# Windowed attention on one core: a chunk's turned probability blocks in one PSUM bank and moved by one copy, global probabilities turned once for two units, one-bank buffers, another order of the steps

## The chip, the cores and the metric

The kernel runs on one core of a Trainium2 chip. The metric is the device time of one execution in microseconds. Three runs of the kernel before took 964.0, 966.15 and 966.29 us; the median is 966.15 us. One further execution, of 966.44 us, was profiled; its span in the trace is 964.6 us, at a mean granted TensorE clock of 0.992.

## The reference

Three stages follow one another: attention with a local window and 32 global rows, a gated net, and a net with a rational function. All in float32.

```python
B, H, Sl, Sg, D, window = 4, 8, 512, 32, 64, 32
def sm(s):
    e = np.exp(s - np.max(s, axis=-1, keepdims=True))
    return e / (np.sum(e, axis=-1, keepdims=True) + 1e-09)
k_all, v_all = np.concatenate([k_g, k_l], 2), np.concatenate([v_g, v_l], 2)
out_g = np.matmul(sm(q_g @ k_all.T / 8), v_all)            # 32 global queries see all 544 keys
s_ll  = np.where(abs(i - j) <= window, q_l @ k_l.T / 8, -1e9)
out_l = np.matmul(sm([q_l @ k_g.T / 8, s_ll]), v_all)      # 512 local queries: 32 global keys and a window
x = [out_g, out_l]                                         # 2304 tokens x 512
x = (sigmoid(x @ w_gate) * (x @ w_val)) @ w_out            # d_ff 1536
h = x @ w_in                                               # d_ff 2048
g = P(h) / (Q(h) + 1e-6)                                   # cubic over 1 + |b0||h| + |b1|h^2
out = g @ w_out
```

## The kernel before, in words

The attention is cut into 16 units: 4 batches by 4 pairs of heads. A unit has 512 local queries in four chunks of 128, and two heads, `j` = 0 and 1. Each chunk and head sees 224 keys: its own 128, the 32 global ones and two neighbour strips of 32, so a unit's scores are eight blocks of 128 x 224. The 32 global queries of two heads in two neighbouring units are taken together, in the even unit: 4 x 32 = 128 rows by 544 keys.

The steps of a unit `u`, with the name of the function and the engine:

- `s_mm` (TensorE, L201): scores of half a unit (two chunks) into a buffer `pss` of two PSUM banks. `s_max` (VectorE, L210): one custom instruction for each chunk and head reads the scores, subtracts the mask, writes them into `p` and gives the row's maximum. `s_exp` (ScalarE, L217): the exponential with its row sum. `s_add` (GpSimd, L222) adds 1e-9 to the sums, `s_rec` (VectorE, L226) inverts them, `s_norm` (GpSimd, L231) multiplies a chunk of `p`.
- `g_mm` (L239), `g_max` (VectorE, L245), `g_neg` (GpSimd, L249), `g_exp`, `g_add`, `g_rec` (L263), `g_norm` (L267): the same for the global queries, into `pgn`, in even units only.
- `t_mm` (TensorE, L270): for each chunk the probabilities are turned (transposed) into a two-bank buffer `pspt`. Bank 0 takes the own keys of both heads and the chunk's global probabilities, 320 columns; bank 1 takes the 96 other keys, on 96 partitions. `t_own` (VectorE, L291) copies bank 0 into `to`, `t_edge` (ScalarE, L297) copies bank 1 into `te`.
- `v_own` (L306), `v_edge` (L314): the products with the values, into `po` (in the trace `pspv`), two banks for a unit, local and global outputs side by side.
- `x_hi` (ScalarE, L331) writes the outputs rounded to float32r as `xh`, `x_lo` (VectorE, L335) what the rounding left as `xl`, `x_g` (VectorE, L345) adds up the global outputs of the four chunks into `xga`; `x_out` (GpSimd) writes those into `xh` and `xl` once a batch is done.

The order in which the program is written is a table, `STEPS`, of rows (place, name, arguments). Step `name` of unit `u` is written at `u + place`, all sorted by this number, so several units are under way at once; each engine runs its instructions in that order and waits on semaphores. I call the stretch from the first score read of one unit to that of the next a frame. Between them stand the steps `w_raw` to `w_lo`, which load and convert four of the net's weight blocks (place + 3.5 times the block's number). `load`, `g_load` and `c_load` issue DMAs on SyncE's queue, in the same order. `KEPT` says how many units of keys, queries and values are held.

All PSUM buffers of the attention are of one kind, `pair`: four of two banks each, used in turn by `pss`, `psgl`, `pspt` and `po`. Two readers of one such buffer on different engines follow each other, and a buffer is written again only when all readers are done.

After the attention come `gated` (its first matmul is L491) and the rational net, in which each weight is applied as a high and a low part in three matmuls (L491 to L493).

Of the kernel before, what the change touches and what calls it, by code (L numbers as in the profile page):

```python
# [36 lines left out]
def tile_of(tok):  # L37
# [9 lines left out]
    (-3.305, 'load', 'k'),  # L47
    (-3.124, 'load', 'q'),
    (-2.697, 'g_load'),
    (-2.554, 'c_load', 'masks'),  # L50
    (-1.417, 's_mm', 0),
    (-1.371, 'w_raw'),
    (-1.261, 's_max', 0, 1),
    (-1.208, 's_max', 0, 0),
    (-1.023, 'c_load', 'ident'),
    (-0.771, 's_mm', 1),
    (-0.720, 's_max', 1, 0),
    (-0.718, 's_exp', 0, 0),
    (-0.696, 's_max', 1, 1),
    (-0.542, 's_exp', 0, 1),  # L60
    (-0.456, 'g_mm'),
    (-0.370, 'g_max'),
    (-0.257, 's_add', 0),
    (-0.195, 's_exp', 1, 1),
    (-0.192, 'g_neg'),
    (-0.153, 'g_exp'),
    (0.054, 's_exp', 1, 0),
    (0.156, 'load', 'v'),
    (0.164, 'g_add'),
    (0.164, 's_rec', 0),  # L70
# [24 lines left out]
    (1.766, 'v_own', 1),
    (1.780, 'v_edge', 1),
    (1.783, 't_own', 3),
    (1.860, 't_edge', 3),
    (1.864, 'v_own', 2),
    (1.873, 'x_hi', 0),  # L100
    (1.991, 'v_edge', 2),
    (2.040, 'w_hi'),
    (2.070, 'v_own', 3),
    (2.085, 'v_edge', 3),
    (2.103, 'x_g'),
    (2.171, 'x_hi', 1),
    (2.202, 'x_lo', 0),
    (2.203, 'x_lo', 1),
    (2.461, 'w_lo'),
    (2.494, 'x_out'),  # L110
# [28 lines left out]
KEPT = dict(k=4, q=3, v=3, w=3)  # L139


def attention(ctx, tc, ident, xh, xl, ins, other={}, others=0):
# [3 lines left out]
    ps = ctx.enter_context(tc.tile_pool(name="ps", bufs=4, space=PSUM))  # L146

    def pair(name):

        return ps.tile([128, 2, 512], F32, tag="ps", name=name)  # L150
# [10 lines left out]
    for i in range(2):  # L161
        nc.gpsimd.memset(pgn[i][:, S + SG :], 0.0)
# [10 lines left out]
    def load(u, names):  # L173

        b, pr = units[u]
        for x in names:
            shape = {"k": [128, NBLK, WIN], "w": [EDGE, NBLK, 128]}.get(x, [128, NBLK, 128])
            t = st[u][f"{x}n"] = two.tile(shape, F32, tag=f"{x}n", name=f"{x}n{u}", bufs=KEPT[x])
            nc.sync.dma_start(t, ins[f"{x}_l"][b, pr])

# [8 lines left out]
    def s_mm(u, half):  # L189
# [5 lines left out]
        s["sm", half] = two.tile([128, 4], F32, tag="sm", name=f"sm{u}_{half}", bufs=4)  # L195
# [24 lines left out]
    def s_add(u, half):  # L220
        r = st[u]["r", half] = two.tile([128, 4], F32, tag="r", name=f"r{u}_{half}", bufs=4)
        nc.gpsimd.tensor_scalar_add(r, st[u]["sm", half], 1e-9)  # L222

    def s_rec(u, half):
        r = st[u]["r", half]
        nc.vector.reciprocal(r, r)  # L226

    def s_norm(u, half, i):
        p = st[u]["p"][:, 2 * half + i]
        r = st[u]["r", half][:, 2 * i : 2 * i + 2].unsqueeze(2).to_broadcast([128, 2, WIN])  # L230
        nc.gpsimd.tensor_tensor(p, p, r, ALU.mult)  # L231
# [10 lines left out]
    def g_max(u):  # L242
        s = st[u]
        s["gmx"] = two.tile([128, 1], F32, tag="gmx", name=f"gmx{u}")
        nc.vector.tensor_reduce(s["gmx"], s["psg"], mybir.AxisListType.X, ALU.max)  # L245

    def g_neg(u):
        t = st[u]["gmx"]
        nc.gpsimd.tensor_scalar_mul(t, t, -0.125)  # L249
# [7 lines left out]
    def g_add(u):  # L257
        r = st[u]["gr"] = two.tile([128, 1], F32, tag="gr", name=f"gr{u}")
        nc.gpsimd.tensor_scalar_add(r, st[u]["gsm"], 1e-9)

    def g_rec(u):
        r = st[u]["gr"]
        nc.vector.reciprocal(r, r)  # L263

    def g_norm(u):
        n = pgn[u // 2 % 2][:, 0 : S + SG]
        nc.gpsimd.tensor_tensor(n, n, st[u]["gr"].to_broadcast([128, S + SG]), ALU.mult)  # L267

    def turn(out, src):
        nc.tensor.matmul(out, src, ident, is_transpose=True, start=True, stop=True, skip_group_check=True)  # L270

    def t_mm(u, c):

        s = st[u]
        s["pt", c] = ps = pair(f"pspt{u}_{c}")
        g = pgn[u // 2 % 2]
        gat = 128 if u % 2 == 0 else 64
        turn(ps[:, 0, gat : gat + 128], g[:, c * 128 : (c + 1) * 128])
        turn(ps[:, 0, 0:128], s["p"][:, c, 0, 0:128])
        turn(ps[:, 0, 192:320], s["p"][:, c, 1, 0:128])  # L280
        at = 128
        if c == 0:
            turn(ps[0:EDGE, 1, gat : gat + 128], g[:, S : S + EDGE])
            at = 192
        turn(ps[0:EDGE, 1, 0:128], s["p"][:, c, 0, 128:WIN])
        turn(ps[0:EDGE, 1, at : at + 128], s["p"][:, c, 1, 128:WIN])

    def t_own(u, c):
        s = st[u]
        s["to", c] = t = two.tile([128, 320], F32, tag="to", name=f"to{u}_{c}", bufs=3)  # L290
        nc.vector.tensor_copy(t, s["pt", c][:, 0, 0:320])  # L291

    def t_edge(u, c):
        s = st[u]
        n = 320 if c == 0 else 256
        s["te", c] = t = two.tile([EDGE, 320], F32, tag="te", name=f"te{u}_{c}", bufs=3)
        nc.scalar.copy(t[:, 0:n], s["pt", c][0:EDGE, 1, 0:n])  # L297

    def v_own(u, c):

        s = st[u]
        if c == 0:
            s["po"] = pair(f"pspv{u}")
        for j in range(2):
            rows, at = slice(64 * j, 64 * j + 64), 192 * (c % 2) + 32 * (1 - j)
            nc.tensor.matmul(s["po"][rows, c // 2, at : at + 160], s["vn"][:, c, rows], s["to", c][:, 160 * j : 160 * j + 160],  # L306
                             start=True, stop=False)

    def v_edge(u, c):
        s = st[u]  # L310
        n = 160 if c == 0 else 128
        for j in range(2):
            rows, at = slice(64 * j, 64 * j + 64), 192 * (c % 2) + (32 * (1 - j) if c == 0 else 32)
            nc.tensor.matmul(s["po"][rows, c // 2, at : at + n], s["wn"][:, c, rows], s["te", c][:, n * j : n * j + n],  # L314
                             start=False, stop=True)

    def x_parts(u, half):

        b, pr = units[u]
        for c in range(2 * half, 2 * half + 2):  # L320
# [5 lines left out]
            src = st[u]["po"][:, half, 0:384].rearrange("p (c t) -> p c t", t=192)[:, c % 2 : c % 2 + n, 32:160]  # L326
# [11 lines left out]
    xga = [one.tile([128, NPAIR, SG], F32, name=f"xga{i}") for i in range(2)]  # L338

    def x_g(u):  # L340
        b, pr = units[u]
        for j in range(2):
# [487 lines left out]
```

## Time and profile before

| | us |
|---|---|
| median of three runs | 966.15 |
| profiled execution | 966.44 |
| its span | 964.6 |
| TensorE busy in the span | 926.8 (96%) |
| VectorE busy | 687.8 (71%) |
| ScalarE busy | 579.7 (60%) |
| GpSimd busy | 506.2 (52%) |

The execution's own time is 1.84 us longer than its span. In rows of the trace PE is TensorE's matmuls, PEld its weight loads, DVE VectorE, ACT ScalarE, POOL GpSimd, SP SyncE. A row of the timeline gives the start, the duration, the engine, the line of the program and the tiles, out<-in, of one or (x4) several instructions in a run; its bracket is the idle time of the engine before it and what ended it. The busy shares are means over stages with different limits, so the stages are looked at one by one below.

### The profile page before, as it was taken

How to read it: one execution, taken by the hardware profiler on the slowest of the kernel's cores; microseconds unless marked ns; L12 is line 12 of the kernel's file. 1: busy time of each engine (PE TensorE's matmuls, PEld its weight loads, DVE VectorE, ACT ScalarE, POOL GpSimd, SP SyncE). 2: the span in 40 equal slices, each digit the busy share in tenths (PEclk: the TensorE clock that was granted, in tenths of full speed). 3: DMA queues.
4: the chain of work that ended last, by engine and by line, in shares of the span. 5: the costliest groups of instructions: out<-in, count | busy, mean ns of one | idle time of the engine just before them, and what ended most of it. 6: DMA issues, size and time to landing. Idle time of an engine off the chain costs nothing.

```text
span 964.6 us, 14517 instructions
## 1 busy us (share of the span) xinstructions
PE 926.8 (96%) x5104; PEld 810.0 (84%) x5104; DVE 687.8 (71%) x1324; ACT 579.7 (60%) x1227; POOL 506.2 (52%) x471
## 2 busy tenths in 40 slices
PE   6888888999999999999999999999999999999996
PEld 4666666898898898898998998898889888988894
DVE  5777763567667676676766238987888789878985
ACT  6777763444444444344444348877778787777773
POOL 4666571354444444444454337544466566655763
PEclk8999999999999999999999999999999999999999
DMA  8455320244344343344443321001300220010111
GB/s 292 137 174 173 102 83 23 87 154 132 131 151 155 120 154 131 122 151 131 131 164 133 119 88 45 1 1 66 109 0 23 71 83 1 28 60 1 66 55 66
DMA packets 51917, 94.42 MB, mean 98 GB/s; under 512 B 4356, under 2 KB 25988, under 8 KB 51844
## 3 DMA queue, kind: packets, MB, share of 16 engines
q1 hardware_dynamic: 51844, 93.49, 29.2%
q8 instruction: 40, 0.66, 0.3%
q14 instruction: 33, 0.27, 0.1%
HBM read 72.24 MB, written 21.23 MB: 97 GB/s over the span
## 4 chain that ended last, share of the span: by engine, by line
PE 83%; DVE 6%; ACT 5%; issue 3%; POOL 2%; DMA 0%; SPq 0%; ACTq 0%; DVEq 0%; POOLq 0%
PE rp L685 6%; PE rp L684 6%; PE rp L683 6%; PE rp L493 6%; PE rp L491 6%; PE rp L492 6%; PE pg L492 5%; PE pg L491 5%; PE pg L493 5%; PE pv L493 5%; PE pv L492 5%; PE pv L491 5%; PE p L536 5%; PE p L535 5%; PE p L534 5%
## 5 line engine op out<-in xcount | busy, mean ns | idle before, releaser
L615 POOL TENSOR_TENSOR v<-v,u 128x384 f32<-128x384 f32 (+1 forms) x80 | 96.5, 1206 | 112.6 <-ACT v L611 112.0
L658 POOL TENSOR_TENSOR rgl<-t,rgh 128x384 fp32r<-128x384 f32 (+1 forms) x80 | 96.3, 1204 | 37.3 <-POOL v L615 30.5
L522 ACT CAST gh<-t 128x384 fp32r<-128x384 f32 (+1 forms) x60 | 33.4, 557 | 124.7 <-DVE t L519 123.0
L519 DVE TENSOR_TENSOR t<-pv,t 128x384 f32<-128x384 f32 (+1 forms) x60 | 36.6, 610 | 78.3 <-PE pv L493 74.4
L623 DVE TENSOR_TENSOR t<-rp,t 128x384 f32<-128x384 f32 (+1 forms) x80 | 48.6, 608 | 54.4 <-ACT t L619 53.6
L608 ACT ACTIVATE u<-rp 128x384 f32<-128x384 f32 (+1 forms) x80 | 42.6, 533 | 65.7 <-PE rp L493 65.6
L644 DVE SCALAR_TENSOR_TENSOR v<-v,u 128x384 f32<-128x384 f32 (+1 forms) x80 | 79.1, 988 | 0.0
L648 DVE SCALAR_TENSOR_TENSOR t<-t,co,v 128x384 f32<-128x384 f32 (+1 forms) x80 | 74.1, 926 | 2.8
L231 POOL TENSOR_TENSOR p<-p,r 128x448 f32<-128x448 f32 x64 | 59.6, 938 | 17.7 <-DVE r L226 15.2
L523 DVE TENSOR_TENSOR gl<-t,gh 128x384 fp32r<-128x384 f32 (+1 forms) x60 | 39.5, 658 | 37.4 <-ACT gh L522 37.4
L217 ACT ACTIVATE p<-p,mx 128x224 f32<-128x224 f32 x128 | 60.7, 479 | 6.1 <-DVE mx L210 6.1
L611 ACT ACTIVATE v<-u,co 128x384 f32<-128x384 f32 (+1 forms) x80 | 60.3, 753 | 2.7
L632 ACT ACTIVATE u<-v,co 128x384 f32<-128x384 f32 (+1 forms) x80 | 52.7, 659 | 9.8 <-POOL v L615 9.7
L546 DVE TENSOR_TENSOR gacc<-p,gacc 128x384 f32<-128x384 f32 (+1 forms) x100 | 54.8, 603 | 4.6 <-PE p L536 4.6
L619 ACT ACTIVATE t<-rp,co 128x384 f32<-128x384 f32 (+1 forms) x80 | 55.9, 698 | 0.0
L640 DVE SCALAR_TENSOR_TENSOR v<-v,u 128x384 f32<-128x384 f32 (+1 forms) x80 | 55.3, 692 | 0.0
L627 DVE SCALAR_TENSOR_TENSOR t<-t,co,rp 128x384 f32<-128x384 f32 (+1 forms) x80 | 52.8, 660 | 0.0
L210 DVE CUSTOM_DVE_ANT_0 p<-pss,masks 128x224 f32<-128x224 f32 x128 | 43.0, 385 | 13.2 <-DMA masks<-in_masks 7.1
L636 ACT ACTIVATE u<-u,co 128x384 f32<-128x384 f32 (+1 forms) x80 | 51.9, 648 | 0.0
L654 ACT CAST rgh<-t 128x384 fp32r<-128x384 f32 (+1 forms) x80 | 43.5, 544 | 5.9 <-DVE t L648 5.9
L201 PE MATMUL pss<-kn,qn 64*128 64x224 f32 x256 | 34.6, 395 | 8.7 <-DMA qn<-in_q_l 6.1
L270 PE MATMUL pspt<-ident,p 128*128 128x128 f32 (+1 forms) x256 | 40.8, 280 | 0.0
(564 smaller groups left out, 3133.7 us busy)
## 6 DMA issues: line engine op xcount, KB each, us to landing
raw2in<-in_w_in SPq DMA_DIRECT2D x16, 512.0 KB, 3.7
raw2out<-in_w_out SPq DMA_DIRECT2D x16, 512.0 KB, 3.4
kn<-in_k_l SPq DMA_DIRECT2D x16, 448.0 KB, 4.9
raw1gate<-in_w_gate SPq DMA_DIRECT2D x12, 512.0 KB, 5.4
raw1val<-in_w_val SPq DMA_DIRECT2D x12, 512.0 KB, 3.7
raw1out<-in_w_out SPq DMA_DIRECT2D x12, 512.0 KB, 3.4
out<-racc SPq DMA_DIRECT2D x17, 256.0 KB, 2.0
qn<-in_q_l SPq DMA_DIRECT2D x16, 256.0 KB, 2.7
```

Source lines behind the costliest of these rows:

```text
L217: nc.scalar.activation(p, p, AF.Exp, bias=s["mx", half][:, n : n + 1], scale=-1.0, accum_out=s["sm", half][:, n : n + 1])
L231: nc.gpsimd.tensor_tensor(p, p, r, ALU.mult)
L491: nc.tensor.matmul(ps, wh[:, w], mh[:, k], start=k == 0, stop=False)
L492: nc.tensor.matmul(ps, wh[:, w], ml[:, k], start=False, stop=False)
L493: nc.tensor.matmul(ps, wl[:, w], mh[:, k], start=False, stop=k == 3)
L611: nc.scalar.activation(new(u, "v"), st[u]["u"], AF.Identity, bias=b0, scale=b1)
L615: nc.gpsimd.tensor_tensor(s["v"], s["v"], s["u"], ALU.mult)
L644: nc.vector.scalar_tensor_tensor(s["v"], s["v"], 2.0, s["u"], ALU.subtract, ALU.mult)
L648: nc.vector.scalar_tensor_tensor(s["t1"], s["t1"], a0, s["v"], ALU.add, ALU.mult)
L658: nc.gpsimd.tensor_tensor(s["gl"], s["t1"], s["gh"].bitcast(F32), ALU.subtract)
L683: nc.tensor.matmul(ps, gh[:, w], wh, start=k == 0, stop=False)
L684: nc.tensor.matmul(ps, gh[:, w], wl, start=False, stop=False)
```

## The change

The turned blocks. `t_mm` makes four turns of 128 columns for a chunk, two of the own keys and two of keys 96 to 223, into one bank of a new kind of buffer, `bank` (four of one bank; `pair` now has two). Its second two thus have 128 rows, of which the first 32 repeat own keys; the value tile `wn` has zeros there, in three static tiles. One copy of 512 columns, `t_out`, moves the bank into `to`, on ScalarE for chunks 1 and 3 and on VectorE for 0 and 2.

The global probabilities are turned once for two units (`g_turn`, five turns into two banks) and copied into `to` by `e_own` (VectorE, two copies of 128 columns a unit) and `e_edge` (ScalarE, one of 64 columns).

The outputs of a unit's halves lie in a bank each; `x_g` is a copy of 32 columns for each half, and the two halves are added on GpSimd in `x_out`. The small operations `s_add`, `g_neg` and `g_add` go from GpSimd to VectorE, ahead of the reciprocals and behind the global maximum. All places in `STEPS` are new, the loads' among them.

```diff
-    (-3.305, 'load', 'k'),
-    (-2.554, 'c_load', 'masks'),
+    (-3.328, 'c_load', 'masks'),
+    (-2.228, 'load', 'k'),
...
-    ps = ctx.enter_context(tc.tile_pool(name="ps", bufs=4, space=PSUM))
+    ps = ctx.enter_context(tc.tile_pool(name="ps", bufs=2, space=PSUM))
+    def bank(name):
+        return ps.tile([128, 512], F32, tag="bank", name=name, bufs=4)
+    wn = [one.tile([128, NBLK, 128], F32, name=f"wn{i}") for i in range(3)]
+    for t in wn:
+        nc.gpsimd.memset(t[0 : 128 - EDGE], 0.0)
...
-    def s_add(u, half):
-        r = st[u]["r", half] = two.tile([128, 4], F32, tag="r", name=f"r{u}_{half}", bufs=4)
-        nc.gpsimd.tensor_scalar_add(r, st[u]["sm", half], 1e-9)
     def s_rec(u, half):
-        r = st[u]["r", half]
+        r = st[u]["sm", half]
+        nc.vector.tensor_scalar_add(r, r, 1e-9)
         nc.vector.reciprocal(r, r)
...
+        nc.vector.tensor_scalar_mul(t, t, -0.125)
-    def g_neg(u):
-        t = st[u]["gmx"]
-        nc.gpsimd.tensor_scalar_mul(t, t, -0.125)
...
     def g_rec(u):
-        r = st[u]["gr"]
+        r = st[u]["gsm"]
+        nc.vector.tensor_scalar_add(r, r, 1e-9)
         nc.vector.reciprocal(r, r)
...
+    def g_turn(u):
+        g = pgn[u // 2 % 2]
+        st[u]["go"], st[u]["ge"] = bank(f"psgo{u}"), bank(f"psge{u}")
+        for c in range(NBLK):
+            nc.tensor.transpose(st[u]["go"][:, c * 128 : (c + 1) * 128], g[:, c * 128 : (c + 1) * 128], ident)
+        nc.tensor.transpose(st[u]["ge"][:, 0:128], g[:, S - 128 + EDGE : S + EDGE], ident)
+    def e_own(u):
+        src = st[u - u % 2]["go"].rearrange("p (c h g) -> p c h g", c=NBLK, h=4)[:, :, 2 * (u % 2) : 2 * (u % 2) + 2]
+        for i in range(2):
+            nc.vector.tensor_copy(turned(u)[:, i::2, 0:2, 128 * (1 - i) : 128 * (1 - i) + SG], src[:, i::2])
+    def e_edge(u):
+        at = 64 * (u % 2)
+        src = st[u - u % 2]["ge"][:, at : at + 64].rearrange("p (h g) -> p h g", h=2)
+        nc.scalar.copy(turned(u)[:, 0, 2:4, 128:160], src)
     def t_mm(u, c):
-        s["pt", c] = ps = pair(f"pspt{u}_{c}")
...
+        s["pt", c] = ps = bank(f"pspt{u}_{c}")
+        for j in range(2):
+            nc.tensor.transpose(ps[:, 128 * j : 128 * j + 128], s["p"][:, c, j, 0:128], ident)
+        for j in range(2):
+            nc.tensor.transpose(ps[:, 256 + 128 * j : 384 + 128 * j], s["p"][:, c, j, EDGE:WIN], ident)
-    def t_own(u, c):
-        nc.vector.tensor_copy(t, s["pt", c][:, 0, 0:320])
-    def t_edge(u, c):
-        nc.scalar.copy(t[:, 0:n], s["pt", c][0:EDGE, 1, 0:n])
+    def t_out(u, c):
+        at = SG * (c % 2)
+        src = st[u]["pt", c].rearrange("p (n k) -> p n k", n=4)
+        (nc.scalar.copy if c in T_ACT else nc.vector.tensor_copy)(turned(u)[:, c, :, at : at + 128], src)
     def v_own(u, c):
-        if c == 0:
-            s["po"] = pair(f"pspv{u}")
+        if c % 2 == 0:
+            s["po", c // 2] = bank(f"pspv{u}_{c // 2}")
...
-    def x_g(u):
-            nc.vector.tensor_reduce(xga[b % 2][rows, pr], src, mybir.AxisListType.XY, ALU.add)
+    def x_g(u, half):
+        nc.vector.tensor_copy(xga[b % 2][:, pr, half], st[u]["po", half][:, 128:160])
     def x_out(u):
+            nc.gpsimd.tensor_tensor(g[:, :, 0], g[:, :, 0], g[:, :, 1], ALU.add)
```

The first place is VectorE between the score reads of unit 4 (`pss4`) and of unit 5 (`pss5`); the number behind `to`, `pspt`, `pspv`, `mx`, `r`, `sm` and `p` is the unit, `gmx4` belongs to the global queries of units 4 and 5. Before:

```order
L210 ISA p4_431,mx4_1_503<-pss4_1_502,masks_89 128x224
L210 ISA mx4_1_503 128x1
L291 COPY to2_2_538<-pspt2_2_524 128x320
L245 TENSOR_REDUCE gmx4_564<-psgl4_546 128x1
L226 RECIPROCAL r3_1_531<-r3_1_531 128x4
L210 ISA p5_551,mx5_0_553<-pss5_0_552,masks_89 128x224
```

and now:

```order
L248 TENSOR_REDUCE gmx4_515<-psgl4_502 128x1
L249 TENSOR_SCALAR gmx4_515<-gmx4_515 128x1
L282 COPY to3_522<-psgo2_391 128x2x2x32 x2
L228 TENSOR_SCALAR sm3_1_362<-sm3_1_362 128x4
L229 RECIPROCAL sm3_1_362<-sm3_1_362 128x4
L340 TENSOR_TENSOR xl0_72<-pspv2_0_510,xh0_67 128x256
L347 COPY xga0_102<-pspv2_0_510 128x32
L228 TENSOR_SCALAR sm4_0_441<-sm4_0_441 128x4
L229 RECIPROCAL sm4_0_441<-sm4_0_441 128x4
L259 TENSOR_SCALAR gsm4_539<-gsm4_539 128x1
```

The copies of the turned blocks no longer stand here one by one between the reads; all small operations of a unit stand together, ahead of the next unit's reads.

The second place is TensorE from the value products of unit 2 on. Before:

```order
L306 MATMUL pspv2_561<-to2_3_583,vn2_370 64x160 x2
L314 MATMUL pspv2_561<-te2_3_592,wn2_416 64x128 x2
L270 MATMUL pspt3_0_613<-ident_66,pgn1_91 128x128
L270 MATMUL pspt3_0_613<-ident_66,p3_304 128x128 x2
L270 MATMUL pspt3_0_613<-ident_66,pgn1_91 96x128
L270 MATMUL pspt3_0_613<-ident_66,p3_304 96x128 x2
L270 MATMUL pspt3_1_628<-ident_66,pgn1_91 128x128
L270 MATMUL pspt3_1_628<-ident_66,p3_304 128x128 x2
L270 MATMUL pspt3_1_628<-ident_66,p3_304 96x128 x2
L201 MATMUL pss5_1_636<-kn5_321,qn5_346 128x224 x4
```

and now:

```order
L310 MATMUL pspv2_1_529<-to2_416,vn2_398 64x160 x2
L318 MATMUL pspv2_1_529<-to2_416,wn2_94 64x128 x2
L207 MATMUL pss5_0_548<-kn5_430,qn5_446 128x224 x4
L294 MATMUL pspt3_0_565<-ident_66,p3_321 128x128 x2
L296 MATMUL pspt3_0_565<-ident_66,p3_321 128x128 x2
L294 MATMUL pspt3_1_574<-ident_66,p3_321 128x128 x2
L296 MATMUL pspt3_1_574<-ident_66,p3_321 128x128 x2
L207 MATMUL pss5_1_584<-kn5_430,qn5_446 128x224 x4
```

A chunk now has four turns instead of five (six in chunk 0), the turns of `pgn` are gone from here, and the scores of unit 5 stand behind the products of unit 2 instead of among the turns ahead of them.

The third place is the start of SyncE's queue. Before:

```order
L179 DMA kn0_98<-in_k_l 128x896
L179 DMA qn0_100<-in_q_l 128x512
L184 DMA qgn0_102<-in_q_g 128x128
L187 DMA masks_89<-in_masks 128x672
L179 DMA kn1_105<-in_k_l 128x896
L179 DMA qn1_107<-in_q_l 128x512
L416 DMA raw1gate0_117<-in_w_gate 128x4x256
```

and now:

```order
L193 DMA masks_89<-in_masks 128x672
L184 DMA kn0_105<-in_k_l 128x896
L184 DMA qn0_107<-in_q_l 128x512
L190 DMA qgn0_109<-in_q_g 128x128
L184 DMA kn1_111<-in_k_l 128x896
L184 DMA qn1_121<-in_q_l 128x512
```

The masks went to the front and the first weight block back, behind the start.

## Rows read from the trace of the kernel before

**Rows 1.** Busy by stage: length, PE, PEld, DVE, ACT, POOL (instructions), clock, DMA, GB/s.
```profile
16.23:154.44 138.21, 119.16 (x1119) 89.59 (x1118) 98.06 (x410) 96.16 (x354) 88.08 (x129) 0.98 0.42 132
154.44:964.60 810.16, 799.94 (x3936) 714.17 (x3936) 580.91 (x876) 474.11 (x842) 413.09 (x328) 1.00 0.26 88
```

**Rows 2.** Waits, 24 to 140 us: total, times, longest.
```profile
ACT te L297 <- DVE to L291: 19.0, 21, 1.3
DVE xga L345 <- PE pspv L314: 14.0, 11, 1.4
ACT xh L331 <- DVE xga L345: 9.5, 12, 1.3
```

**Rows 3.** Chain of waits, 24.9 to 42.7 us: start, time, piece.
```profile
25.00 0.41 DVE to L291
...
35.30 0.28 DVE xga L345
...
35.98 0.38 ACT xh L331
...
42.18 0.40 DVE to L291
```

**Rows 4.** L210 alone (eight score reads), 7.05 to 9.55 us: length, DVE, clock, DMA.
```profile
7.05:9.55 2.50, 2.50 (x16) 1.00 1.06 390
```

**Rows 5.** Timeline: VectorE's copies from PSUM, 320 and 512 columns.
```profile
142.50 1.28 DVE L291 COPY to<-pspt 128x320 f32<-128x320 f32 x3
...
177.38 2.48 DVE L544 COPY gacc<-p 128x512 f32<-128x512 f32 x4
```

**Rows 6.** VectorE's groups, 24 to 140 us: busy, mean ns, idle before.
```profile
L226 DVE RECIPROCAL r<-r 128x4 f32<-128x4 f32 x27 | 4.7, 173 | 0.4
L245 DVE TENSOR_REDUCE gmx<-psgl 128x1 f32<-128x544 f32 x6 | 4.3, 724 | 4.7 <-PE psgl L239 4.7
```

**Rows 7.** Timeline at the attention's end: last rest, first matmul of the gated net.
```profile
153.54 0.76 DVE L335 TENSOR_TENSOR xl<-pspv,xh 128x256 fp32r<-128x256 f32 x2 [0.49 <-ACT xh L331]
...
154.44 0.56 PE L491 MATMUL pg<-xh,w10gate 128*128 128x512 f32 x1 [2.10 <-DVE xl L335]
```

**Rows 8.** Timeline of TensorE: scores and value products.
```profile
119.55 1.03 PE L201 MATMUL pss<-kn,qn 64*128 64x224 f32 x8 [0.43 <-ACT te L297]
120.50 0.49 PE L306 MATMUL pspv<-to,vn 128*64 128x160 f32 x4
...
121.59 0.44 PE L306 MATMUL pspv<-to,vn 128*64 128x160 f32 x4
```

**Rows 9.** Timeline: turns on TensorE at the full clock.
```profile
117.71 0.60 PE L270 MATMUL pspt<-ident,p 128*128 128x128 f32 x4
...
118.73 0.38 PE L270 MATMUL pspt<-ident,p 128*96 128x128 f32 x2
```

**Rows 10.** ScalarE's exponentials (groups, 24 to 140 us).
```profile
L217 ACT ACTIVATE p<-p,mx 128x224 f32<-128x224 f32 x105 | 49.9, 481 | 0.0
```

**Rows 11.** Timeline: ScalarE's copy of 512 columns.
```profile
613.65 1.06 ACT L700 COPY racc<-rp 128x512 f32<-128x512 f32 x2
```

**Rows 12.** Timeline of VectorE and GpSimd: an operation from SBUF, alone and beside GpSimd.
```profile
74.66 0.42 DVE L435 TENSOR_SCALAR v1gate<-v1gate 128x512 f32<-128x512 f32 x1
...
75.57 0.69 DVE L437 SCALAR_TENSOR_TENSOR v1gate<-raw1gate,v1gate 128x512 uint32<-128x512 uint32 x1
...
102.81 1.82 POOL L231 TENSOR_TENSOR p<-p,r 128x448 f32<-128x448 f32 x2
...
104.02 0.90 DVE L435 TENSOR_SCALAR v1val<-v1val 128x512 f32<-128x512 f32 x1
```

**Rows 13.** Timeline of VectorE at the start: masks, first read of unit 2.
```profile
7.05 0.39 DVE L210 CUSTOM_DVE_ANT_0 p<-pss,masks 128x224 f32<-128x224 f32 x1 [7.05 <-DMA masks<-in_masks]
...
16.23 0.35 DVE L210 CUSTOM_DVE_ANT_0 p<-pss,masks 128x224 f32<-128x224 f32 x1
```

**Rows 14.** Windows, TensorE early on: length, busy, clock, DMA, GB/s.
```profile
18.27:20.13 1.86, 1.86 (x10) 0.50 0.81 238
```

More of the change, by code (lines that the diff above doesn't have):

```diff
@@ new lines @@
+    (-0.285, 's_exp', 0, 1),
+    (-0.191, 'g_exp'),
+    (-0.145, 'c_load', 'ident'),
+    (0.026, 's_rec', 0),
+    (0.091, 'g_rec'),
+    (0.174, 's_exp', 1, 0),
+    (0.474, 'g_norm'),
+    (0.475, 's_exp', 1, 1),
+    (0.496, 'g_turn'),
+    (0.525, 'load', 'v'),
+    (0.572, 's_norm', 0, 0),
+    (0.596, 's_norm', 0, 1),
+    (0.711, 'e_own'),
+    (0.747, 's_rec', 1),
+    (0.756, 'e_edge'),
+    (0.814, 'load', 'w'),
+    (1.105, 't_mm', 0),
+    (1.193, 'w_raw'),
+    (1.216, 't_mm', 1),
@@ new lines @@
+    (1.293, 's_norm', 1, 1),
+    (1.326, 't_out', 0),
+    (1.359, 's_norm', 1, 0),
+    (1.419, 't_out', 1),
+    (1.439, 't_mm', 3),
+    (1.450, 't_mm', 2),
+    (1.483, 't_out', 3),
+    (1.540, 't_out', 2),
+    (1.616, 'v_own', 0),
+    (1.619, 'v_edge', 0),
+    (1.670, 'v_own', 1),
+    (1.690, 'v_edge', 1),
+    (1.722, 'x_hi', 0),
+    (1.746, 'v_own', 2),
+    (1.765, 'v_edge', 2),
+    (1.811, 'v_own', 3),
+    (1.826, 'v_edge', 3),
+    (1.834, 'x_hi', 1),
+    (1.871, 'w_mag'),
+    (1.944, 'x_lo', 0),
@@ L111 @@
+    (2.009, 'x_g', 0),
+    (2.150, 'x_lo', 1),
+    (2.207, 'x_g', 1),
+    (2.441, 'w_bits'),
+    (3.739, 'w_add'),
+    (3.887, 'w_hi'),
+    (6.602, 'w_lo'),
+    (6.926, 'x_out'),
 ]
@@ L194, in s_mm @@
         s["mx", half] = two.tile([128, 4], F32, tag="mx", name=f"mx{u}_{half}", bufs=4)
-        s["sm", half] = two.tile([128, 4], F32, tag="sm", name=f"sm{u}_{half}", bufs=4)
+        s["sm", half] = two.tile([128, 4], F32, tag="sm", name=f"sm{u}_{half}", bufs=6)
         for i in range(2):
@@ new lines, in turned @@
+    def turned(u):
+        if "to" not in st[u]:
+            st[u]["to"] = two.tile([128, NBLK, 4, 160], F32, tag="to", name=f"to{u}", bufs=3)
+        return st[u]["to"]
+    def e_own(u):
[6 more added lines that the diff above has]
+        nc.scalar.copy(turned(u)[:, 0, 2:4, 128:160], src)
@@ L312, in v_edge @@
         for j in range(2):
-            rows, at = slice(64 * j, 64 * j + 64), 192 * (c % 2) + (32 * (1 - j) if c == 0 else 32)
-            nc.tensor.matmul(s["po"][rows, c // 2, at : at + n], s["wn"][:, c, rows], s["te", c][:, n * j : n * j + n],
-                             start=False, stop=True)
+            rows, at = slice(64 * j, 64 * j + 64), 160 * (c % 2)
+            nc.tensor.matmul(s["po", c // 2][rows, at : at + n], wn[u % 3][:, c, rows],
+                             turned(u)[:, c, 2 + j, SG * (c % 2) : SG * (c % 2) + n],
+                             start=False, stop=c % 2 == 1, skip_group_check=True)
     def x_parts(u, half):
@@ L364, in attention @@
         last = 1 if name == "c_load" else others if name in other else n
-        order += [(u * (SPREAD if name in other else 1) + place, name, u, args) for u in range(last) if name[0:2] != "g_" or u % 2 == 0]
+        order += [(u * (SPREAD if name in other else 1) + place, name, u, args) for u in range(last)
+                  if name[0:2] != "g_" or u % 2 == 0]
     for _, name, u, args in sorted(order, key=lambda step: step[0]):
```

143 lines of the change are left out of this document (36 added, 107 removed).

## The prediction

> **What bounds the kernel now.** I read the busy time by stage first. From 154.44 us on TensorE is busy 799.94 of 810.16 us [rows 1]: nothing in that stage can start earlier than its inputs, and it runs at TensorE's own pace. The change touches the stretch before it, and what this gains or loses should shift the rest. There TensorE is busy 119 of 138 us, and VectorE, ScalarE and GpSimd 88 to 98 each: no engine is full, so the attention is bound by waits between engines.
>
> The waits name them [rows 2]. ScalarE's copy of the edge block waits for VectorE's copy of the own block, which reads the same two-bank buffer: 19.0 us in all. VectorE's global sum waits 14.0 us for the value products, and ScalarE's rounding of the local outputs, which reads the same buffer as that sum, 9.5 us. The chain of waits shows them in line: an own copy at 25.00, later the global sum at 35.30 and the rounding at 35.98, and the same kind of copy again at 42.18 [rows 3]. Two units (an even and an odd one, since global queries come every second time) take 42.18 - 25.00 = 17.18 us.
>
> **The change part by part: a new list for VectorE.** The own and edge copies, global sums and their waits go; I write down what VectorE does for two units afterwards.
>
> - Sixteen score reads: eight take 2.50 us, .31 each [rows 4], so 5.0.
> - Four copies of 512 columns. The trace shows copies of 320 columns .40 apart ((1.28 - .48)/2, with .48 the last one's own time) and of 512 columns .62 apart (2.48/4) [rows 5]. 4 x .62 = 2.5. The new ones write strips of 128; I take the same.
> - Four copies of 128 columns for the global part, two a unit. No such row exists. Below, the reciprocal of four columns takes .17 [rows 6]; above, the 320 columns' .40. The straight line through 320 and 512 gives .18, near the lower end, so I take .2: .8.
> - Four rests `x_lo` at .38 (.76 for two) [rows 7]: 1.5. Four copies of 32 columns, .1 by the same line: .4; their upper end is the sum that they replace, .28 [rows 3], which would add .7.
> - Four times the add ahead of the reciprocal, now on VectorE. Reciprocal .17 [rows 6] and an add of the same shape, taken alike: .35, in all 1.4. Once the global maximum .72 [rows 6] and three operations of one column at about .16: 1.2.
>
> Together 12.8 us of work. By walking the two engine orders against each other I find two waits left where VectorE stands idle: .35 for ScalarE's rounding in the odd unit and .2 for the last turned block. 13.4.
>
> **TensorE and ScalarE beside it.** TensorE: scores of four halves, .95 each from one start to the next instruction's (119.55 to 120.50) [rows 8], 3.8. Turns: 32 of a chunk's blocks and five global ones, 37 instead of 42; two more take .60 - .38 = .22 [rows 9], .11 each, 4.1; with the last one's tail counted every time (.60/4) it were .15, 5.6, but tails overlap. A global score step has 2176 columns where a half's scores have 1792: 1.2. Value products of two chunks 121.59 - 120.50 = 1.09 [rows 8], of eight 4.4. Together 13.5, at most 15.0. ScalarE: sixteen exponentials at .48 [rows 10], four copies at .53 (1.06/2) [rows 11], four roundings at .38 [rows 3], the global exponential about 1 and two small copies: 12.8. So the three engines come out within 6% of each other, and the 43 us of waits [rows 2] can be collected only until VectorE and TensorE are full: 17.18 to 13.4 at best.
>
> **The price of the moved adds.** GpSimd multiplies `p` while VectorE does its small operations. One row shows what an operation that reads SBUF may pay: 128 x 512 takes .42 alone, but .90 where GpSimd's multiplication runs from 102.81 to 104.63; it ends just behind it [rows 12]. The adds of 128 x 4 and 128 x 1, six for two units, had stood on GpSimd, so the trace has no row of them on VectorE. Lower bound: not held at all, as the reciprocals of that size, at a mean of .173 [rows 6], are not. Upper bound: each waits for a whole multiplication, .91 [rows 12], 5.5 for two units. If they met GpSimd at random (eight multiplications and a global one, 8.4 of 14 us, so .6 of the time, half of one left) it were .6 x .46 x 6 = 1.7. In the new order two of the four 128 x 4 adds stand just where GpSimd has begun to multiply by the reciprocal before, so I take .75, nearer to the row of the reciprocals: 14.15.
>
> The Trainium skill ("SBUF — State Buffer", Who interferes with whom) says that VectorE in a two-port mode and GpSimd exclude each other for a whole instruction, whoever is first; that agrees with the .90. By the Trainium skill ("VectorE: DVE Perf Modes", Mode 2×_2P — use both read ports for one tensor) the mode splits an even outermost dimension, which an add of four columns has and one of a single column has not; by that four of the six adds can be held, and the period would lie between 13.4 and 17.0. No run so far shows it at this size.
>
> **GpSimd and the queues.** GpSimd loses six small operations and has 8.4 of 14; it is not the bound. The masks' DMA (128 x 672, 344 KB) goes ahead of the first keys and queries; at 390 GB/s [rows 4] that is .9 us at the start, though the first score read waited for just these masks until 7.05 [rows 13]. I take the whole .9, the upper bound; the lower is 0. The first weight block is behind the start now, which helps the keys. The keys come about one unit ahead of their use instead of two; at 132 GB/s [rows 1] there is room, so I put nothing on it.
>
> **The sum, along the start of each frame.** First read of unit 2: 16.23 [rows 13] + .9 = 17.1. First frame: TensorE's 6.7 us, but the granted clock was .50, the level of 1.2 GHz, from 18.27 to 20.13 [rows 14]; between 7.1, half a period, and 13.4, TensorE's time at that level, I take the middle, 10.2. Thirteen frames, 6.5 x 14.15 = 92.0. Four weight blocks: three operations, .42 + .42 + .69 [rows 12], on VectorE, now full, and some of it held: 2 each, 8.0. The end: turns and products of units 14 and 15, 7.8 on TensorE, two copies exposed at .53, and the 2.1 us from the last product to the gated net [rows 7]: 11.0. Together 138.3 against 154.44: 16.1 saved. 966.44 - 16.1 = 950.3 for the profiled execution, which stands .3 above the median: 950.
>
> **The rivals.**
>
> - No add is held (the reciprocals' row speaks for it). Thirteen frames 87.1, weights 1.5 each, 6.2: 131.6, 22.8 saved: 944.
> - The adds meet GpSimd at random, and the three nearly full engines wait for each other some .4 more: 15.5, so 100.8: 147.1, 7.3 saved: 959. For it: the lists differ by less than 1 us, and every buffer is handed on between them. Against: four buffers of one bank, where turned blocks had shared four with everything else.
> - No change. The copy of 512 columns stands in front of the products: TensorE waits for ScalarE's last copy at the first half and VectorE's at the second. If 1.6 us of that lay bare in each unit, 3.2 for two, the period were 16.6, and 16.6 is (154.44 - 17.1 - 10.2 - 8 - 11)/6.5, the break-even. Against: scores and the global step stand between turns and products in even units. 966.
> - Slower: the hold decides. Every one of the six adds, standing in VectorE's one line, is held for a whole multiplication and the reads queue behind it. Scores, exponentials and copies all follow from VectorE, so nothing covers it: 13.4 + 5.5 = 18.9, 122.9 for the frames, 169.2: 15 more, 981. It decides from a mean hold of (16.6 - 13.4)/6 = .53 us on. For it: the one row in which both meet, where more than half was lost. Against: .53 is over the random .28.
>
> **How the numbers follow.** Forecast .43, no hold .20, random hold .20, no change .08, slower .09. The forecast's own range is 946 to 956, from the small copies' bounds (-.1 and +1.5 for two units), the start and the first frame. About .3% (2.9 us) is what a measurement of this kernel can tell from no change. Faster .83, the same .08, slower .09. The range from 942 to 962 takes in the first three cases and leaves out the last two.
>
> **What would show it.** Right: the gated net's first matmul near 138.3, the waits of `te` for `to` and of `xga` gone, two units in about 14 us with VectorE busy over 90%, adds of 128 x 4 partly near .6 while GpSimd multiplies, those of 128 x 1 short, a copy of 512 columns at .62, the stage behind at 810 us. Wrong: VectorE idle for over 2 us in two units (a wait took the place), adds of .9 throughout, or a later stage longer than before.

## The result, and the profile after

The changed kernel takes 942.79 us (median of four runs, 942.24 to 943.63), the kernel before 965.08 in the same comparison: a ratio of 0.977 (0.975 to 0.979). Run again beside the last three experiments it took 942.62, a ratio of 0.9765 (0.9752 to 0.9778). The profiled execution took 943.63 us with a span of 941.4, 23.2 less than the span before. Of the 41 executions of the kernel before that ran beside the experiments, 16 took 963.6 to 964.8 us at a mean granted clock of .996 and 25, like the profiled one, 965.8 to 968.1 at .992 to .994, so some 2 us of what two single traces differ by need not be in every execution.

Busy time by stage, as in [rows 1]: up to the first score read of unit 2, the first frame (that of unit 2), the thirteen others, the end, the nets (length, PE, PEld, DVE, ACT, POOL, clock, DMA share, GB/s):

```profile
0.00:16.87 16.87, 9.10 (x59) 6.58 (x60) 7.61 (x44) 8.10 (x29) 4.98 (x14) 1.00 0.92 318
16.87:24.01 7.14, 7.14 (x75) 5.49 (x74) 7.00 (x33) 7.01 (x26) 5.10 (x6) 1.00 0.76 232
24.01:122.93 98.92, 92.41 (x907) 71.83 (x905) 93.70 (x405) 83.12 (x303) 66.49 (x73) 0.98 0.50 163
122.93:133.38 10.45, 8.16 (x92) 7.00 (x93) 5.41 (x17) 5.06 (x15) 6.51 (x10) 1.00 0.01 2
133.38:941.40 808.02, 798.32 (x3936) 712.97 (x3936) 580.96 (x876) 473.97 (x842) 414.29 (x331) 1.00 0.26 88
```

The nets start at 133.38 instead of 154.44, 21.1 us earlier, and take 808.02 instead of 810.16, another 2.1. In the thirteen frames VectorE is now busy 93.7 of 98.9 us and TensorE 92.4.

The waits from 24 to 125 us that answer to [rows 2] (total, times, longest):

```profile
POOL p L234 <- DVE sm L229: 26.8, 12, 3.8
ACT to L301 <- PE pspt L296: 8.8, 8, 2.7
...
ACT xh L336 <- PE pspv L318: 6.1, 11, 1.5
```

None of the three waits of [rows 2] is left in them. The largest is GpSimd's, which has room. A fourth wait of before is gone too, and it is one of TensorE's own. In the kernel before (24 to 140 us) it read:

```profile
PE pspv L314 <- ACT xh L331: 9.3, 14, 1.3
```

The value products of a unit's second half waited there for ScalarE's rounding of the first half, which lay in the same two-bank buffer. From 16.23 to 154.44 this wait is 10.2 of the 19.05 us in which TensorE is idle. [Rows 2] leave it out and the prediction does not name it; the change removes it by giving each half a bank of its own. No run tests that part by itself.

The chain of waits from 32 to 47 us, where [rows 3] had copies, sums and roundings in turn, lies nearly whole on TensorE; these are pieces of an even unit (start, time, piece):

```profile
32.53 0.41 PE pspt L294 x2
32.94 0.22 PE pspt L296 x2
33.15 0.96 PE pss L207 x8
...
35.13 1.10 PE psgl L242 x8
36.23 0.30 PE pspv L310 x4
```

And two frames without weight conversion, even and odd. I call such two a clean pair:

```profile
32.30:39.88 7.58, 7.35 (x75) 5.75 (x76) 7.14 (x33) 6.51 (x23) 5.09 (x6) 1.00 0.71 229
39.88:46.06 6.18, 6.18 (x67) 5.12 (x66) 5.87 (x30) 5.78 (x22) 4.51 (x6) 1.00 0.56 179
```

Together 13.76 us, where two units took 17.18 [rows 3]. The window of those two units, before:

```profile
25.00:42.18 17.18, 15.21 (x148) 11.35 (x146) 12.31 (x56) 12.86 (x48) 10.93 (x17) 1.00 0.49 147
```

TensorE's idle time went from 1.97 to .23 and its work from 15.21 to 13.53: of the 3.42 us that a pair gained, about half is waiting and half is less work on TensorE, which has fewer turns to make. TensorE is now busy 13.53 us of the pair and VectorE 13.01. The two are within half a microsecond of each other, so the rows alone do not say which of them sets the pace.

VectorE's groups, 24 to 125 us, which answer to [rows 5, 6] (busy, mean ns, idle before):

```profile
L301 DVE COPY to<-pspt 128x512 f32<-128x512 f32 x27 | 18.5, 687 | 2.4 <-PE pspt L296 2.4
...
L228 DVE TENSOR_SCALAR sm<-sm 128x4 f32<-128x4 f32 x26 | 10.7, 412 | 0.0
...
L282 DVE COPY to<-psgo 128x128 f32<-128x128 f32 x26 | 6.2, 282 | 0.0
```

The adds of 128 x 4 took .412 us on average. The timeline around one of them tells why; GpSimd first, then VectorE:

```profile
38.14 1.83 POOL L234 TENSOR_TENSOR p<-p,sm 128x448 f32<-128x448 f32 x2 [2.49 <-DVE sm L229]
```

```profile
37.62 0.17 DVE L228 TENSOR_SCALAR sm<-sm 128x4 f32<-128x4 f32 x1
...
38.32 0.78 DVE L228 TENSOR_SCALAR sm<-sm 128x4 f32<-128x4 f32 x1
39.13 0.18 DVE L229 RECIPROCAL sm<-sm 128x4 f32<-128x4 f32 x1
39.23 0.12 DVE L259 TENSOR_SCALAR gsm<-gsm 128x1 f32<-128x1 f32 x1
```

The add at 37.62 runs before GpSimd starts and takes .17. The one at 38.32 meets the first of GpSimd's two multiplications and ends just behind it (38.14 + .92 = 39.06, the add at 39.10). The reciprocal and the add of one column at 39.13 and 39.23 run inside the second multiplication and are not held. All 128 x 1 adds of L259 took .12 to .16, and six of the eight lie inside a multiplication. Those of L228 took .15 to 1.08.

The Trainium skill ("VectorE: DVE Perf Modes", Mode 2×_2P — use both read ports for one tensor) says that the mode splits the outermost dimension that is longer than one, which must be even, or odd and equal for source and destination. Four columns can be split so; that a single column cannot is my reading of it. By that an add of four columns can be held and the add of one column cannot, and the rows agree.

TensorE around the start of the nets, as windows (length, busy, clock, DMA share, GB/s), before and then after:

```profile
152.34:154.44 2.10, 0.00 (x0) 1.00 0.00 0
154.44:156.50 2.06, 2.06 (x6) 0.56 0.00 0
```

```profile
132.26:133.38 1.12, 0.00 (x0) 1.00 0.00 0
133.38:135.40 2.02, 2.02 (x9) 1.00 0.00 0
```

Behind 2.10 us of idleness the granted clock was .56, near its lower level of 1.2 GHz; behind 1.12 it stayed at 2.4 GHz. That is where the 2.1 us in the nets come from: in the eleven traces of this case in which the clock stays up there, the nets take 807.9 to 808.1 us, and in the three in which it falls 809.7 to 810.5.

The changed kernel lost the clock in another place. In the profiled execution TensorE was idle for 1.67 us in the attention, and the clock was .50 soon after:

```profile
105.52:107.19 1.67, 0.00 (x1) 1.00 0.76 272
...
109.00:112.40 3.40, 3.40 (x16) 0.50 0.00 0
```

In the trace of a second execution of the same kernel (the run "again" below) the same idle time stands in the same place, and the clock stayed:

```profile
105.89:107.55 1.66, 0.01 (x2) 1.00 0.72 263
...
109.55:111.55 2.00, 2.00 (x16) 1.00 0.00 0
```

The frame there took 9.05 us in the first and 7.62 in the second; the frames around it took the same in both, so the 1.4 us are put down to the clock. So the length of an idle stretch does not by itself decide whether the clock falls.

### The profile page after: what moved, and what is told of

It reads as the page before. It is cut to its first block, busy times and chain, and to the rows that moved or that the text cites. A ratio compares the mean times of both kernels' runs of the same rounds, so it can differ in the third digit from the quotient of the medians.

```text
span 941.4 us, 14394 instructions
## 1 busy us (share of the span) xinstructions
PE 915.1 (97%) x5064; PEld 803.9 (85%) x5064; DVE 694.7 (74%) x1372; ACT 577.3 (61%) x1211; POOL 497.4 (53%) x430
## 4 chain that ended last, share of the span: by engine, by line
PE 85%; DVE 8%; ACT 2%; issue 1%; POOL 1%; DMA 0%; SPq 0%; DVEq 0%; POOLq 0%
PE rp L689 6%; PE rp L688 6%; PE rp L687 6%; PE rp L497 6%; PE rp L495 6%; PE rp L496 6%; PE pg L497 5%; PE pg L495 5%; PE pg L496 5%; PE pv L497 5%; PE pv L495 5%; PE pv L496 5%; PE p L540 5%; PE p L539 5%; PE p L538 5%; DVE p L216 2%
## 5 line engine op out<-in xcount | busy, mean ns | idle before, releaser
L234 POOL TENSOR_TENSOR p<-p,sm 128x448 f32<-128x448 f32 x64 | 58.8, 944 | 34.6 <-DVE sm L229 30.5
L446 POOL TENSOR_TENSOR v2in<-v2in,q2in 128x512 uint32<-128x512 uint32 x16 | 20.7, 1292 | 38.4 <-DVE v2in L441 38.4
```

## The experiments

**The adds left out, and the adds on GpSimd.** Was VectorE's list, with the held adds, the pace?

```diff
     def s_rec(u, half):
         r = st[u]["sm", half]
-        nc.vector.tensor_scalar_add(r, r, 1e-9)
+        nc.gpsimd.tensor_scalar_add(r, r, 1e-9)   # second run; in the first the line is gone
         nc.vector.reciprocal(r, r)
```

> The changed kernel without the add of 1e-9 ahead of the local reciprocals (128 x 4, four for two units); the sums are at least 1, so nothing else differs. In the changed kernel these adds take .412 us each on average, those held .78, and two units take 13.76 us. Theory: VectorE and TensorE are both nearly full (26.0 and 27.1 of 27.5 us in four frames), so about 1.5 us of VectorE's list go but TensorE stops the gain at about .5 for two units: some 3 us, 939 to 941. Rival: VectorE alone sets the pace, then 6.5 x 1.5 = 10 us, 933. Second rival: the adds lie beside TensorE's work anyway: no change, 943.

> The changed kernel with the four local adds back on GpSimd, in the same places of the order. Theory: VectorE loses 1.4 us of list and the hold, but each reciprocal now waits for GpSimd, whose queue has multiplications of .94 in it; TensorE is nearly full besides: 940 to 944, so the move of the adds is worth next to nothing. Rival (the hold is costly): as without the add, 933 to 940. Rival (the wait for GpSimd's queue is costly, as in the kernel before): two units .5 to 1.5 longer, 946 to 953.

Measured 937.27 and 937.39, both a ratio of 0.9705 (0.9688 to 0.9722 and 0.9723): some 5.4 us below the changed kernel. The gain is larger than my theory's 3, and it does not lie where I put it. Two frames without the adds, and the two that follow, with a weight block in the first:

```profile
31.60:38.70 7.10, 7.10 (x74) 5.47 (x73) 6.48 (x30) 6.26 (x23) 5.18 (x6) 1.00 0.74 234
38.70:45.38 6.68, 6.68 (x71) 5.62 (x70) 5.51 (x27) 6.28 (x24) 5.07 (x7) 1.00 0.59 196
...
45.38:54.69 9.31, 9.31 (x92) 7.19 (x90) 8.87 (x34) 8.74 (x31) 3.98 (x5) 1.00 0.58 209
54.69:60.20 5.51, 5.09 (x53) 3.84 (x52) 5.26 (x27) 4.22 (x17) 5.51 (x6) 1.00 0.58 179
```

The first two take 13.78, the same as with the adds, though VectorE is busy 11.99 instead of 13.01; TensorE is busy throughout. So VectorE is not the pace there. The next two take 14.82; in the changed kernel the same two take 16.74:

```profile
46.06:55.78 9.72, 9.55 (x92) 7.19 (x90) 9.21 (x35) 9.02 (x33) 4.25 (x6) 1.00 0.61 216
55.78:62.80 7.02, 5.37 (x53) 4.04 (x53) 6.95 (x30) 4.87 (x17) 6.63 (x7) 1.00 0.62 202
```

The weight block's three VectorE operations stand in the first of these frames. In the second, 55.78 to 62.80, VectorE is busy 6.95 of 7.02 and TensorE only 5.37: VectorE is the pace, and both of its adds are held there, the first by a weight operation on GpSimd (GpSimd, then VectorE):

```profile
59.65 1.26 POOL L446 TENSOR_TENSOR v1val<-v1val,q1val 128x512 uint32<-128x512 uint32 x1
```

```profile
59.86 1.08 DVE L228 TENSOR_SCALAR sm<-sm 128x4 f32<-128x4 f32 x1
...
61.48 0.78 DVE L228 TENSOR_SCALAR sm<-sm 128x4 f32<-128x4 f32 x1
```

Against .16 alone the two are held for .92 + .62 = 1.54 us, and without them the frame is 1.51 shorter (5.51 for 7.02). On GpSimd the adds cost nothing that can be measured: that part of the change loses some 5 us. How much of this is the hold and how much the adds' own time, the two runs do not separate.

**The one copy made two again.** For all four chunks:

```diff
     def t_out(u, c):
-        (nc.scalar.copy if c in T_ACT else nc.vector.tensor_copy)(turned(u)[:, c, :, at : at + 128], src)
+        nc.vector.tensor_copy(turned(u)[:, c, 0:2, at : at + 128], src[:, 0:2])
+        nc.scalar.copy(turned(u)[:, c, 2:4, at : at + 128], src[:, 2:4])
```

> The changed kernel with each chunk's one copy of 512 columns made two copies of 256, the own half on VectorE and the edge half on ScalarE, for all four chunks, out of the same bank. VectorE's work for a unit stays about the same (four of .33 against two of .60), ScalarE's too (four of .36 against two of .56). Theory (the kernel before was bound by one engine's copy waiting for the other's in the same buffer): ScalarE waits for VectorE again at every chunk, two units take 14.5 to 16, 948 to 958. Rival (only the engines' lists count): .13 for a unit, 943 to 946.

Measured 949.19, ratio 0.9828 (0.9811 to 0.9846): 6.4 us more. The wait is back:

```profile
ACT to L302 <- DVE to L301: 16.9, 19, 2.8
...
PE pspv L311 <- ACT to L302: 7.3, 7, 2.6
```

Two frames take 14.59 (34.80 to 49.39), with VectorE busy 12.78 and ScalarE 12.80 of it, nearly as before the split (13.01 and 12.29). The theory holds: it is two readers of one buffer in a row that cost. Not all of the 6.4 us is the wait itself. One frame takes 10.5 us instead of 8.3; TensorE was idle for 2.59 us in it and its clock fell to .50 behind that.

**All copies on VectorE.**

```diff
-T_ACT = (1, 3)
+T_ACT = ()
```

> The changed kernel with all four copies of a unit on VectorE. Theory (VectorE's list is full): 2 x .60 more for each of 16 units, 17 to 20 us more, 960 to 963. Rival (TensorE or the waits set the pace, VectorE has room): at most 5 us more, 943 to 948.

Measured 960.36, ratio 0.9941 (0.992 to 0.9963): 17.6 us more. VectorE has no room for them; two frames take 15.66, with VectorE busy in 15.45 of it. Without the copies' division between two engines little of the gain is left. Part of the loss is TensorE's clock, which fell to .50 three times in the attention, at idle times of 1.96 to 3.39 us.

**The masks back behind the first keys.**

```diff
-    (-3.328, 'c_load', 'masks'),
     (-1.621, 'g_load'),
+    (-1.5, 'c_load', 'masks'),
```

> The changed kernel with the masks' DMA back behind the first keys, queries and global queries; the other loads stay. In the changed kernel the first score read starts at 8.15, the read of unit 2 at 16.87 and TensorE keeps a granted clock of 1.00 through the first frame (24.01); in the kernel before the clock was .50 from 16.23 on. Theory of the prediction (masks ahead cost .9): the read of unit 2 at 16.0, .5 to 1 us less, 942. Theory of the clock (TensorE kept its level since the matmuls of the start stand closer): if the masks are what did it, the clock falls again and the first frame takes 2 to 3 us more, 945. Rival: neither, 943, and the clock stays at 1.00.

Measured 941.73, ratio 0.975 (0.9735 to 0.9765). That overlaps with the changed kernel's interval, so the size stays open. In the trace unit 2's first read stands at 15.64 instead of 16.87, but this place moves from execution to execution: in the eight traces with the masks ahead and the other loads as in the changed kernel it lies between 16.23 and 17.52, and in the two with the masks back at 15.48 and 15.64. The clock stays at 1.00 through the first frame (15.64 to 22.78, 7.14). The masks' place is not what keeps the clock. What differs ahead of that frame is TensorE's idle time. Before, the first turns waited for the global probabilities, and the clock was at .50 from 14.7 to 21.6:

```profile
15.73 0.48 PE L270 MATMUL pspt<-ident,pgn 128*128 128x128 f32 x1 [2.40 <-POOL pgn L267]
```

In the changed kernel the longest idle time from 11 to 24 us is .82. That this is the cause is argued from the two traces; no run tests it.

**The last global sum of the kernel before, later.**

```diff
+        late = 0.11 if name == "x_g" else 0
-        order += [(u * (SPREAD if name in other else 1) + place, name, u, args)
+        order += [(u * (SPREAD if name in other else 1) + place + late * (u == n - 1), name, u, args)
```

> The kernel before with one change: the global sum of the last unit stands behind its two rests on VectorE, where it stood ahead. In the kernel before TensorE is idle for 2.10 us ahead of the gated net and its granted clock is .56 to .60 for the next 4 us; in the changed kernel it is idle for 1.12 and stays at 1.00. Theory (the shorter idle time keeps the clock, which is worth about 2 us of the stage behind): idle 1.1 to 1.5, clock 1.00, stage behind 808, in all 2.5 to 3 us less than before, 963. Rival (the clock falls for another reason): .7 us less, 965.4, stage behind still 810.

Measured 966.26, ratio 1.0001 (0.9989 to 1.0012): no change, and my theory missed. The idle time fell only to 1.85, since the first matmul then waits for the sum itself, and the clock fell all the same (.51 from 155 to 157 us).

**The nets started later.**

```diff
-            nc.vector.tensor_tensor(l, src, h.bitcast(F32), ALU.subtract)
+            for _ in range(4 if u == len(units) - 1 and half else 1):
+                nc.vector.tensor_tensor(l, src, h.bitcast(F32), ALU.subtract)
```

> The changed kernel with the last rest of the last unit computed four times over, so that the gated net starts later and TensorE is idle for 1.0 longer, 2.1 in all as in the kernel before. Theory (the idle time there decides the clock): the granted clock falls to near .56 at the gated net's start and the stage behind takes 2 us more, 3 us in all, 946. Rival (the clock has another reason): 1.0 us more, 944, clock 1.00.

Measured 946.11, ratio 0.9799 (0.9783 to 0.9815): 3.3 us more. TensorE there:

```profile
131.71:134.20 2.49, 0.00 (x1) 1.00 0.00 0
134.20:136.20 2.00, 2.00 (x7) 0.75 0.00 0
```

The idle time is 1.4 longer and the nets take 943.9 - 134.2 = 809.7 us instead of 808.0. The clock's fall thus costs 1.7 us beside the delay, as the theory says. Of these four cases, 1.12 us kept the level and 1.85, 2.10 and 2.49 lost it. That is no limit, though. The two runs on parts and order below show, at the start of the nets and in the attention:

```profile
190.55:192.40 1.85, 0.00 (x0) 1.00 0.00 0
192.40:194.40 2.00, 2.00 (x9) 1.00 0.00 0
```

```profile
85.23:88.28 3.05, 0.01 (x1) 1.00 0.97 325
88.28:90.28 2.00, 2.00 (x19) 1.00 1.02 349
```

The first is the old functions in the new order: 1.85 us again, but the level is kept and the nets take 807.9. The second is the new functions in the old order, where even 3.05 us kept it. What decides beside the idle time stays open here.

**The global turns made twice.**

```diff
+        for _ in range(2):
             for c in range(NBLK):
                 nc.tensor.transpose(st[u]["go"][:, c * 128 : (c + 1) * 128], g[:, c * 128 : (c + 1) * 128], ident)
             nc.tensor.transpose(st[u]["ge"][:, 0:128], g[:, S - 128 + EDGE : S + EDGE], ident)
```

> The changed kernel with the five global turns of two units made twice over, as many turns as if each unit made its own; everything else as it was. Theory (TensorE is full along with VectorE, as two units take 13.8 us with or without the adds): five turns at .11 are .55 for two units, 7 to 8 times, 3.5 to 4.5 us more, 946 to 947. Rival (VectorE alone sets the pace and TensorE has .3 to .7 left in two units): 0 to 2 us, 943 to 945.

Measured 945.26, ratio 0.9789 (0.9773 to 0.9804), 2.5 more, between the two. The trace divides them:

```profile
33.45:41.03 7.58, 7.36 (x75) 5.75 (x76) 7.14 (x33) 6.51 (x23) 5.08 (x6) 1.00 0.72 228
41.03:48.02 6.99, 6.99 (x74) 5.85 (x72) 6.29 (x30) 6.17 (x24) 4.90 (x7) 1.00 0.50 162
```

The odd frame, in which the turns stand, grows from 6.18 to 6.99: TensorE is the pace there. Two odd frames grow so, and the first frame grows by .5 (7.65 for 7.14); the other odd frames, with or just behind weight work, stay as they were (7.03 for 7.02, 6.17 for 6.17). So turning once for two units is worth .8 in a clean pair, and in all some 2.5.

**The parts and the order, each alone.** The new functions with the table of before (the copies of the global turns at their new places, the global turns themselves just behind the multiplication that they need, the small copies around the rests), and the old functions with the new table (each copy pair at the place of the one copy, the adds just ahead of the reciprocals).

```diff
-    (-2.228, 'load', 'k'),
-    (1.326, 't_out', 0),
+    (-3.305, 'load', 'k'),
+    (1.213, 't_out', 0),
+    (0.526, 'g_turn'),
+    (2.2025, 'x_g', 0),
...
```

```diff
-    (1.213, 't_own', 0),
-    (1.247, 't_edge', 0),
+    (1.326, 't_own', 0),
+    (1.327, 't_edge', 0),
+    (2.207, 'x_g'),
...
```

> The changed kernel's functions (one bank and one copy for a chunk, shared global turns, one-bank outputs, adds on VectorE) in the order of the kernel before: the same places for all steps that both have; the global turns and their copies at the changed kernel's places, the copies of 32 columns around the rests. Theory (waits between engines inside one buffer bound the kernel before, and these parts remove them): more than half of the 23 us stays, 945 to 954. Rival (the order does it): less than a third, 958 to 966. The old order has a unit's loads, and its first weight block, earlier than the new one.

> The kernel before's functions in the changed kernel's order: each chunk's two copies at the place of its one copy, the adds on GpSimd just ahead of the reciprocals, the global sum at the place of the second small copy. Theory (the order alone can't remove the wait of one copy for the other, and its places fit other steps): 960 to 975. Rival (the order does it): 943 to 955.

Measured 967.39, ratio 1.0025 (1.0008 to 1.0042), and 999.76, ratio 1.0357 (1.0337 to 1.0377). For the parts the theory fell, since more than half of the gain was to stay and none did; for the order alone the loss is larger than the 960 to 975 expected. As placed here, neither gains by itself. TensorE's largest wait in the first, from 24 to 140 us:

```profile
PE psgo L270 <- POOL pgn L264: 13.9, 6, 3.0
```

TensorE stands in line for the global probabilities: the turn for two units has to be done all at once, and at my place for it the multiplication on GpSimd was not done. The clock fell with the waits, to .983 to .993 on average. This is one placing; a better one within the old order was not tried, so the run does not show what the parts are worth in a fitting old order. Waits of the second:

```profile
POOL gmx L249 <- DVE gmx L245: 34.7, 6, 7.9
ACT te L297 <- DVE to L291: 34.3, 30, 2.5
...
PE pspv L306 <- ACT xh L331: 25.7, 10, 3.9
```

Here the copy's wait has grown from 19.0 [rows 2] to 34.3. The line that bears on the time is the last, since it is TensorE's: 25.7 us, where before it was 9.3. In the new order the value products of a unit's second half are written right behind the rounding of its first half (1.722 and 1.746 in the table), and with both halves in one two-bank buffer they have to wait for it. So the new order rests on outputs in two single banks. The clock fell with the waits, to .973 to .980 on average. How much of the loss is this wait and how much the copies, the run does not separate.

**The changed kernel again, and a version from the findings.**

```diff
-        nc.vector.tensor_scalar_add(r, r, 1e-9)   # in s_rec and in g_rec
-    (-3.328, 'c_load', 'masks'),
+    (-1.5, 'c_load', 'masks'),
```

> The changed kernel itself, beside the next three on the same chip: 942 to 944, a ratio of .974 to .979 to the kernel before. It is the base for them.

> The changed kernel without the adds of 1e-9, local and global (the sums are at least 1), and with the masks' DMA behind the first keys and queries. Without the local adds it took 937.3, with the masks back 941.7 instead of 942.8. Theory (both gains add, since one lies in the start and one in the frames): 935.5 to 937. Rival (TensorE is full, the start's gain is lost in its line): 937 to 938.

Measured 942.62 and 936.29, ratios 0.9765 (0.9752 to 0.9778) and 0.9705 (0.9691 to 0.972). The version beats both kernels, by 6.3 us the changed one. Against the kernel without the local adds (0.9705 too) the masks' place and the global adds show nothing that can be measured.

## Why the prediction was right, and where its numbers came from elsewhere

The forecast was 950, the time 942.8. That is inside the range of 942 to 962, but only just, and outside the forecast's own 946 to 956. The direction was right, and so was the mechanism that waits inside shared buffers go and the engines' lists become the bound. Which engine's list it is was half wrong, and several terms were.

- *The waits go, and the engines' lists become the bound.* Right: 17.18 became 13.76, for 14.15 forecast, with the waits gone and the split copy bringing one of them back. What the prediction did not see is that about half of the gain in a pair is less work on TensorE (15.21 to 13.53), and that TensorE's own largest wait, 9.3 us for the rounding, was a fourth one that it didn't name.
- *VectorE is the bound, 12.8 of work, .6 of waits, .75 of hold.* The size was near, in part by luck; the step that names the engine was half wrong. In clean pairs TensorE sets the pace: without the adds a pair takes as long, with more turns it takes longer. My own list gave TensorE 13.5, for 13.53 measured, and I let the hold decide on VectorE. VectorE is the pace in frames with or behind weight work.
- *The hold of the adds, .75 of at most 5.5.* The mechanism was right: in a clean pair the adds were held .62 in the even frame (.78 for .16, the row at 38.32) and a quarter microsecond in the odd, near .9 in all. But it cost nothing in clean pairs; the adds, hold and own time together, cost 5.4 us over the whole, in the other frames.
- *The copies.* 512 columns .60 from start to start (forecast .62), 128 columns .20, 32 columns .10: as forecast.
- *Start.* Unit 2's read at 16.87, forecast 17.1. With the masks moved back it stood 1.3 earlier on average, for the .9 that I had put on them.
- *First frame, 10.2.* Mis-sized by 3.1: it took 7.14. I carried the low clock of [rows 14] over and took the middle between half a period and TensorE's work at the lower level, but TensorE was at its full level there. The trace of before would have told better: with the low clock in most of it (.67 on average), its own first frame took 24.29 - 16.23 = 8.06.
- *Thirteen frames and the weights, 92.0 + 8.0.* 98.92. The sum is near, the split less so: 6.5 times 13.76 is 89.4, which leaves 9.5 for the weights and what they hold up, 1.4 of it the clock from 109.0 on.
- *The end, 11.0.* 10.45.
- *The nets shift unchanged.* Mis-sized by 2.1: they start at the full clock. [Rows 7] show the idle time of 2.10, and I didn't look at the clock behind it. The profiled execution of before is one in which the clock fell there.

The differences sum up: -.2 - 3.1 - 1.1 - .5 = -4.9 to the start of the nets (138.3 against 133.38) and -2.1 behind it, 7.0 in all; around its span the profiled execution has .4 more than before, which leaves the 6.7 between 950.3 and 943.6. The two terms that hang on TensorE's clock are 5.2 of it, so most of the miss is the clock and not the list. The rival without a hold came nearest with 944, but its reason did not hold: the adds were held.

## What to carry to other kernels

A wait inside a buffer with two readers is worth more than the engines' shares show, but the parts and the order of work have to be made for each other: as placed here, neither gained alone. Read first the waits of the engine that is nearest to full; here its largest one was not among those that were named. When several engines come out within a few per cent, work out each stage with its own extra work: moving small operations onto an engine was free where it wasn't the pace and cost 5 us where it was. Ask what the clock is before and after each idle stretch that the change shortens, and look at more than one execution before a microsecond or two is put down to it.

## What the runs showed of the hardware

A VectorE add of 128 x 4 in place, .16 alone, that starts while a GpSimd operation on two operands runs takes until the end of it, in all 14 cases of the changed kernel's trace: up to .78 beside a multiplication of `p`, 1.08 beside the 1.26 us of a weight operation. A reciprocal of 128 x 4 (.18) and an add of 128 x 1 (.12) inside a multiplication do not wait.

TensorE's granted clock stayed at 1.00 behind 1.12 us of idleness ahead of the nets and fell behind 2.10 and 2.49 us, which cost the nets 1.7 to 2.5 us. Between and beyond, the same idle time went either way: 1.66 and 1.67 us in the same place of the same kernel, 1.85 ahead of the nets in two kernels, and 3.05 us once kept the clock.
